# Tile h of one pair of chunks in the space of later sums, and a new order of the instructions from there on

## The chip, the cores and the metric

The kernel runs on one core of one Trainium2 chip. The metric is device time in microseconds. The engines are TensorE (PE, and PEld for its weight loads), VectorE (DVE), ScalarE (ACT), GpSimd (POOL) and SyncE (SP), which issues most transfers. All arithmetic of the products is in float32; the trace holds two records for most products.

## The reference

```python
def _attn_ref(q, k, v, a_re, a_im):            # 4 batches, 8 heads, 768 steps, 48 wide
    mag = np.sqrt(a_re * a_re + a_im * a_im)
    scale = np.minimum(mag, 0.999) / (mag + 1e-06)
    ...
    for t in range(S):
        new_re = ar * S_re - ai * S_im
        new_im = ar * S_im + ai * S_re
        S_re, S_im = new_re + k_t v_t^T, new_im
        y[:, :, t] = q_t @ S_re

def _moe_ref(x, U, V, w_ch1, w_ch2):           # x is y as (4, 768, 384); w_ch1 is 384 x 1536
    u = x + ((x^T @ U) @ V)^T                  # U is 768 x 32
    return u + np.maximum(u @ w_ch1, 0.0) @ w_ch2
```

A gated linear recurrence with complex gates is followed by a mixer over tokens of low rank and a mixer over channels.

## The kernel before, in words

The sequence of each of the four batches is cut into six chunks of 128 tokens. For every chunk the gates are turned into magnitudes and angles (`gates`), q and k are scaled and turned (`prep`, products `tr`), and the attention is computed in pieces (`chain`: products `inner`, `corners`, `dk`, `y`; states `G` and `GM`). Once a batch's six chunks are there, `mixer(m)` takes them as three pairs: m = 0, 1, 2 for the first batch, up to m = 11. A mixer multiplies by U (`rank`) and V (`mixed`), turns u (`uTp`, tile `uT`), forms the up products into tile `h` (1536 x 256 as 128 x 12 x 256), and the "down" products with w2.

There are three ways of doing the up products. For m = 0 they start before U's share is known, and six small products `fix` are then added to h by VectorE (`put_right`). For m = 1 and 2 they are plain (`up`, 36 products of 256 columns each). From m = 3 on they are done with fewer products (`up_fewer`, tile `few`) from sums of blocks of w1, which `combine` makes once, by thirteen VectorE additions of 128 x 512 (L1288): into seven slices of tile `sums` (`sums_w`, 128 x 3584 numbers) and one block of w1 itself. `down` serves m = 0 and `down_two`, with sums of halves of h in tiles `stage` and `more`, the others. Tile h is the single buffer `H_ALL` for all twelve pairs, as a ring of one: a pair's h may be written once the last one's is read for good.

Two steps stand around the place of the change. The weights come as raw words and are converted on the chip: for each of six pieces of w2 ScalarE makes two passes and VectorE three (L587, L400 on `w`, L589). Only then the "down" products of m = 0 that read that piece can run.

The order of all instructions is a table, `ORDER`: for each engine, kind of step and rank it gives the places in one common row of numbers. `plan.order()` sorts by it, and checks that nothing comes before what it needs and no buffer is taken early. A second table, `BANKS`, says which pair of PSUM banks each tile of sums uses. A third, `SPARE`, names places at which TensorE is given products of the identity with itself that nobody reads (L1528, in function `idle`), in units of 128 columns and at most three units to a product.

Of the kernel before, what the change touches and what calls it, by code (L numbers as in the profile page):

```python
# [30 lines left out]
    "TTTTTTTTTTTTTTTTTTAAAAYYYYTTAAAAYYYYTTAAAAYYYYTTAAAAYYYYTTTTTTTTTTAAAAYYYMTTAAAATYTYTTMMMMATAYTYATYMTYMMTYYTTATYTYMMYAYT"  # L31
    "YMTTYAMMMMTTATMTAAYTTATMAYTYAAYYMTTYTAYYTMTYTTAYMTATTYTAATYTMAAYTYAYTYTAYTYTYYYTAYMTTAMYYYAAMYYATTYYTTMTTAYYTMMYTTATYAMA"
    "AAMYTTMMTTTMMTAATAATMTAAYAYTAYAYTAYYTYAMTMYAYYMYAYTYAAMMAYTMYYYTMTYATMAMYATMYMTYTAYTAATAYAYYAAAATYTTAAYMYMYYMMTAAYMMAAYM"
    "TTMMMYYYMMYATYYAYTTYTYATAYTAATYYMTYMAAMTMTAMTATYMYTMAMTMMTYYTYAAYAYTATYTTYTTTYTATAYYTYYTAAMTYYYMMTAYTYTYAAAMTAYYMMTYYTT")
# [20 lines left out]
        ('ACT', 'gates'): {0: [1, 2, 4, 6, 7, 16, 17, 22, 23, 29, 28, 45, 70, 71], 1: [24, 27, 38, 39, 41, 42, 46, 47, 65, 64, 67, 68], 2: [129, 108,  # L55
# [10 lines left out]
        ('DVE', 'gates'): {0: [5, 8, 13, 18, 19, 54, 49], 1: [30, 21, 40, 43, 44, 51, 50], 2: [111, 143, 156, 185, 169], 4: [277, 322, 323, 372, 356],  # L66
# [10 lines left out]
        ('ACT', 'angles'): {0: [72, 86, 98, 100, 103], 1: [76, 106, 112, 114, 126], 2: [210, 231, 251, 240, 241, 242, 263, 269, 271], 4: [375, 395,  # L77
# [5 lines left out]
        ('DVE', 'angles'): {0: [81, 89], 1: [87, 107], 2: [211, 232, 252], 4: [376, 402, 425], 6: [581, 590, 591, 597, 617, 620, 660], 8: [695, 721,  # L83
# [167 lines left out]
def kernel(  # L251
# [812 lines left out]
    def mixer(m):  # L1064
# [120 lines left out]
        def c_of(n):  # L1185
            return "sums_w", n
# [411 lines left out]
```

## Time and profile before

| | |
|---|---|
| median of 3 runs | 617.83 us (615.37, 617.83, 617.84) |
| profiled execution | 616.25 us, span 614.5 us |
| TensorE busy | 597.1 us (97%) |
| VectorE busy | 531.4 us (86%) |
| ScalarE busy | 399.6 us (65%) |
| first `few` product of m = 3 | starts at 266.5 us |
| granted TensorE clock, mean | 0.999 |

A row of a timeline gives the start, the length of the merged records, the engine, the line, what is written from what, and how many records. A row of windows gives for each stretch its length, and for each engine the busy time and the number of its records, then the granted clock and the share and rate of the transfers. A row of waits gives who waited for whom, the total, how often, and the longest. TensorE's records overlap, so that the length of a merged row can be more than the distance to the next start.

### The profile page before, as it was taken

To read this page: it belongs to the slowest core of one execution; us is meant where nothing else is said; L and a number is where in the kernel's file an instruction comes from. 1 tells how busy PE (TensorE), PEld (TensorE's weight loads), DVE (VectorE), ACT (ScalarE), POOL (GpSimd) and SP (SyncE) were. 2 spreads that over 40 slices of the span, in tenths; PEclk is the share of its full clock that TensorE was granted. 3 is DMA by queue.
4 is the path that set the end of the run, shared out by engine and by line. 5 is a ranking of instruction groups with operands and counts; after the bars stand their busy time and mean duration, and the time that the engine had idled before them with its cause. 6 is when DMAs were issued, how large, how long until landed. Compare 5 with 4: busy or idle time off the path is not lost.

```text
span 614.5 us, 23950 instructions
## 1 busy us (share of the span) xinstructions
PE 597.1 (97%) x10572; PEld 526.5 (86%) x10572; DVE 531.4 (86%) x967; ACT 399.6 (65%) x789; POOL 36.9 (6%) x76
## 2 busy tenths in 40 slices
PE   6898989999999999999999999999999999999998
PEld 3566767666889889899999999899999998999997
DVE  6999999999999999999999999889699986464653
ACT  6999999888878898787686876574563532202020
POOL 4000000000000010010100000000100000000010
PEclk9999999999999999999999999999999999999999
DMA  9865556627233534441521522601122200000010
GB/s 212 196 149 119 135 119 153 161 61 151 62 60 69 105 67 75 78 98 27 112 53 22 106 50 45 125 11 29 36 59 47 56 11 19 14 8 7 7 39 26
DMA packets 173687, 45.77 MB, mean 74 GB/s; under 512 B 167632, under 2 KB 170384, under 8 KB 173584
## 3 DMA queue, kind: packets, MB, share of 16 engines
q1 hardware_dynamic: 171376, 39.90, 31.6%
q0 software_dynamic: 2208, 4.35, 2.1%
q8 instruction: 83, 1.36, 0.9%
q14 instruction: 20, 0.16, 0.1%
HBM read 33.59 MB, written 4.72 MB: 62 GB/s over the span
## 4 chain that ended last, share of the span: by engine, by line
PE 85%; ACT 7%; DVE 5%; DMA 1%; issue 1%; SPq 0%; DVEq 0%; ACTq 0%
PE down L1369 25%; PE few L1235 20%; PE up L1135 7%; PE dk L1009 4%; PE tr L873 4%; PE y L1048 4%; PE inner L923 3%; PE inner L920 2%; PE y L1040 2%; ACT gate L394 2%; PE tot L751 2%; PE mixed L1102 1%; PE up L1528 1%; PE uTp L1120 1%; PE corners L984 1%
## 5 line engine op out<-in xcount | busy, mean ns | idle before, releaser
L397 DVE TENSOR_TENSOR QK<-QK,T 96x512 f32<-96x512 f32 (+2 forms) x144 | 101.1, 723 | 4.8 <-ACT QK L884 2.3
L1369 PE MATMUL down<-w,h 128*128 128x192 f32 x396 | 72.1, 330 | 0.0
L1243 ACT COPY h<-few 128x512 f32<-128x512 f32 x54 | 31.1, 585 | 60.3 <-PE few L1235 60.2
L394 ACT ACTIVATE gate<-gate 128x768 f32<-128x768 f32 (+1 forms) x82 | 64.5, 796 | 4.9 <-DMA gate<-in_a_re_dram 1.8
L1369 PEld LDWEIGHTS down<-w,h 128*128 128x128 f32 x396 | 64.4, 190 | 1.3 <-issue 0.4
L884 ACT COPY QK<-tr 96x512 f32<-96x512 f32 x96 | 51.0, 586 | 14.2 <-PE tr L873 13.8
L400 DVE TENSOR_TENSOR xo<-down,xo 128x192 f32<-128x192 f32 (+1 forms) x79 | 29.8, 382 | 23.8 <-PE down L1369 23.5
L1135 PE MATMUL up<-uT,w 128*128 128x256 f32 x216 | 50.3, 385 | 0.0
L1235 PE MATMUL few<-stage,w 128*128 128x128 f32 x360 | 46.7, 277 | 0.0
L1135 PEld LDWEIGHTS up<-uT,w 128*128 128x128 f32 x216 | 40.0, 190 | 5.4
L1235 PEld LDWEIGHTS few<-stage,w 128*128 128x128 f32 x360 | 43.3, 192 | 0.3
L397 DVE TENSOR_TENSOR QKC<-qk,cs 128x768 f32<-128x768 f32 x44 | 41.6, 950 | 1.7 <-ACT cs L394 1.1
L1247 DVE CUSTOM_DVE_ANT_1 h<-few,h 128x512 f32<-128x512 f32 x54 | 35.8, 684 | 4.1 <-PE few L1235 3.1
L1235 PE MATMUL few<-stage,sums 128*128 128x128 f32 x288 | 37.4, 276 | 0.0
L400 DVE TENSOR_TENSOR h<-few,h 128x512 f32<-128x512 f32 x27 | 18.3, 685 | 21.7 <-PE few L1235 13.2
L1369 PE MATMUL down<-stage 128*128 128x192 f32 x198 | 36.8, 330 | 0.0
L1235 PEld LDWEIGHTS few<-stage,sums 128*128 128x128 f32 x288 | 35.2, 192 | 0.1
L989 ACT COPY AT<-corners 32x128 f32<-32x128 f32 x96 | 24.2, 255 | 14.9 <-PE corners L984 13.5
L788 POOL DMA_DIRECT2D gate<-F x15 | 12.1, 806 | 355.1 <-DVE F L817 203.1
L1369 PEld LDWEIGHTS down<-stage 128*128 128x128 f32 x198 | 32.3, 190 | 0.9 <-issue 0.6
L873 PEld LDWEIGHTS tr<-ident,QKC 64*96 64x96 f32 x768 | 24.0, 123 | 9.8 <-DVE QKC L397 3.3
L1311 POOL DMA_DIRECT2D out_dram<-xo x32 | 20.3, 677 | 190.3 <-DVE xo L400 112.4
(197 smaller groups left out, 1358.6 us busy)
## 6 DMA issues: line engine op xcount, KB each, us to landing
stage<-in_moe_w_ch_dram SPq DMA_DIRECT2D x12, 768.0 KB, 5.4
qk<-in_q_dram SPq DMA_DIRECT2D x24, 192.0 KB, 3.9
qk<-in_k_dram SPq DMA_DIRECT2D x24, 192.0 KB, 3.4
VP<-in_v_dram SPq DMA_DIRECT2D x24, 192.0 KB, 4.0
gate<-in_a_re_dram SPq DMA_DIRECT2D x22, 192.0 KB, 4.0
gate<-in_a_im_dram SPq DMA_DIRECT2D x22, 192.0 KB, 4.0
AT<-DG SPq DMA_DIRECT2D x96, 32.0 KB, 2.0
T<-E SPq DMA_DIRECT2D x48, 48.0 KB, 2.9
```

The source lines that it names most:

```text
L394: return nc.scalar.activation(out=o, in_=i, func=f, **kw)
L397: nc.vector.tensor_tensor(out=o, in0=a, in1=b, op=OP.mult)
L400: nc.vector.tensor_tensor(out=o, in0=a, in1=b, op=OP.add)
L873: nc.tensor.transpose(out=get(*ps[r])[0:DQ, h], in_=get(*qkc)[at, h * DQ:(h + 1) * DQ], identity=ident[at, at], tile_position=(r * HC, 0))
L884: nc.scalar.copy(out=to, in_=a)
L1009: nc.tensor.matmul(out=get(*dk[r])[x:x + w, h], lhsT=get(*ks)[at, h * DQ + x:h * DQ + x + w], rhs=get(*VPi)[at, h], start=True, stop=True, ...
L1048: nc.tensor.matmul(out=get(*y[u])[side(r, u), p], lhsT=k_of(h, r * HC, HC), rhs=get(*(mid_G if r else ("G", i - 1)))[:, h], start=False, s ...
L1135: nc.tensor.matmul(out=get(*ps)[:, e], lhsT=w1[:, f, (ff + e) * 128:(ff + e + 1) * 128], rhs=get(*uT)[:, f], start=(f == 0), stop=(f == KD ...
L1235: nc.tensor.matmul(out=get(*ps)[:, q], lhsT=w()[:, q * 128:(q + 1) * 128], rhs=v[0](), start=(n == 0 and q == 0), stop=True, skip_group_ch ...
L1243: ACT(c_act(n3 * CH) - 0.045, RU, lambda i=i, k=k: nc.scalar.copy(out=at(i, k), in_=get(*ps)), [ps], [o])
L1247: DVE(c_dve(n3 * CH), RU, lambda i=i, k=k: nc.vector._custom_dve(dve_ops.TENSOR_ADD_SAT, out=at(i, k), in0=get(*ps), in1=at(i, k), s0=math ...
L1369: nc.tensor.matmul(out=get(*to)[:, part], lhsT=x(j), rhs=y[:, j], start=(first and j == 0), stop=(j == KH - 1), skip_group_check=not first)
```

## The change

For m = 1 tile h becomes the first six of the seven slices of `sums` (3072 of 3584 numbers); all other pairs keep `H_ALL`. The sums of up weights can then be written only after h of m = 1 is no longer read, which the plan is told by a write of `("h", 1)` on three of the thirteen additions. And from the conversion of w2 on (place 505 of some 2770) the three tables are new: every engine's order, the banks and the spare products.

```diff
-        ring(h, "h", [H_ALL])
+        if m == 1:
+            ring(h, "h1", [sums_w.rearrange("p n m -> p (n m)")[:, 0:KF * N].rearrange("p (f t) -> p f t", t=N)])
+        else:
+            ring(h, "h", [H_ALL])
...
             def put(n, x, y, op, reads=()):
                 DVE(c_dve(n3), RC, lambda: nc.vector.tensor_tensor(out=c(n), in0=x(), in1=y(), op=op),
-                    [("w1", f) for f in range(KD)] + [c_of(k) for k in reads], [c_of(n)] + [("w1", 2, 0)] * (n == 7))
+                    [("w1", f) for f in range(KD)] + [c_of(k) for k in reads], [c_of(n)] + [("w1", 2, 0)] * (n == 7) + [("h", 1)] * (n in (0, 6) and not reads))
...
-        ('ACT', 'w2'): {0: [513, 507], 2: [575, 543], 4: [588, 602], 6: [630, 649], 8: [652, 655], 10: [707, 706]},
+        ('ACT', 'w2'): {0: [510, 517], 2: [546, 558], 4: [604, 600], 6: [650, 655], 8: [661, 659], 10: [698, 703]},
...
-         1, 352: 2, 436: 1, 592: 3, 604: 2, 614: 1, 627: 3, 640: 1, 643: 1, 647: 1, 662: 1, 685: 1, 712: 1, 719: 1, 724: 2}
+         1, 352: 2, 436: 1, 585: 3, 605: 2, 618: 3, 620: 1, 628: 1}
```

TensorE, from the spare product ahead of `fix` to the gate products that follow the first "down" products of m = 0 (`w_67` is w2, `ident` the identity of a spare product, GS the gates' logarithms in two parts). Before:

```order
L1528 MATMUL fix<-ident 128x128
L1174 MATMUL fix<-V,rw 128x256 x12
L1528 MATMUL down<-ident 128x384
L806 MATMUL ph<-GS_91,prefix_r 128x384
L806 MATMUL ph<-GS_92,prefix_r 128x384
L1326 MATMUL down<-w_67,h 128x384 x2
L1528 MATMUL ef ps<-ident 128x128
L1326 MATMUL down<-w_67,h 128x384 x6
L1528 MATMUL ef ps<-ident 128x128
L1326 MATMUL down<-w_67,h 128x384 x2
L1528 MATMUL ef ps<-ident 128x128
L1326 MATMUL down<-w_67,h 128x384 x2
```

And now:

```order
L1531 MATMUL ph<-ident 128x384
L806 MATMUL ph<-GS_91,prefix_r 128x384
L806 MATMUL ph<-GS_92,prefix_r 128x384
L1531 MATMUL fix<-ident 128x128
L1177 MATMUL fix<-V,rw 128x256 x12
L1531 MATMUL down<-ident 128x128
L1329 MATMUL down<-w_67,h 128x384 x10
```

The two `ph` products moved ahead of `fix`, ten "down" products stand in a row where twelve were broken up by four spare ones, and behind these rows the change has no spare product any more, where before there were four.

VectorE at the same place, from the first additions of `fix` to h on (`w_67` is w2 in conversion, `w_66` is w1, the rows on gate and GL belong to the next gates). Before:

```order
L1179 ISA h<-fix,h 128x512 x2
L654 ISA gate<-gate 128x768
L1179 ISA h<-fix,h 128x512
L587 TENSOR_SCALAR w_67<-w_67 128x768
L1288 TENSOR_TENSOR sums<-w_66 128x512
L1179 ISA h<-fix,h 128x512
L400 TENSOR_TENSOR gate<-gate 128x768
L1179 ISA h<-fix,h 128x512
L397 TENSOR_TENSOR qk<-qk,es 128x768
L673 SCALAR_TENSOR_TENSOR GL<-GL,gate 128x768
L400 ISA w_67<-w_67,stage 128x1536
L1288 TENSOR_TENSOR sums<-w_66 128x512
```

And now:

```order
L654 ISA gate<-gate 128x768
L1182 ISA h<-fix,h 128x512 x4
L400 TENSOR_TENSOR gate<-gate 128x768
L1182 ISA h<-fix,h 128x512
L687 TENSOR_SCALAR gate<-gate 128x768
L673 SCALAR_TENSOR_TENSOR GL<-GL,gate 128x768
L1182 ISA h<-fix,h 128x512
L587 TENSOR_SCALAR w_67<-w_67 128x768
L683 TENSOR_TENSOR GS_92<-GL,GS_91 128x768
```

The two sums of w1 are gone from here, and the additions to h stand closer together.

VectorE shortly before the first `few` product, the last additions of `combine` in the change (QKC are turned q and k, GM the middle state, `more` the halves of h for "down" of m = 2):

```order
L1291 TENSOR_TENSOR w_66<-w_66 128x512
L1291 TENSOR_TENSOR sums<-w_66,sums 128x512
L397 TENSOR_TENSOR QKC_95<-QKC_95,gate 128x768
L1364 TENSOR_TENSOR more<-h,more 128x384
L1291 TENSOR_TENSOR sums<-sums 128x512
L1291 TENSOR_TENSOR sums<-w_66 128x512
L817 SCALAR_TENSOR_TENSOR F<-F,ph 128x384
L397 TENSOR_TENSOR QKC_93<-qk,cs 128x768
```

Four of the thirteen stand in these rows; in the order before, the last one alone stood ahead of this row of `F`, the two before it some 10 and 20 rows further up.

More of the change, by code (lines that the diff above doesn't have):

```diff
@@ L95 @@
+        ('ACT', 'angles'): {0: [72, 86, 98, 100, 103], 1: [76, 106, 112, 114, 126], 2: [210, 231, 251, 240, 241, 242, 263, 269, 271], 4: [375, 395,
[5 rows of a table added]
+        ('DVE', 'angles'): {0: [81, 89], 1: [87, 107], 2: [211, 232, 252], 4: [376, 402, 425], 6: [582, 583, 584, 594, 614, 616, 658], 8: [694, 724,
[4 rows of a table added]
+        ('DVE', 'prep'): {0: [85, 104, 110], 1: [121, 128, 145], 2: [226, 250, 265], 3: [203, 304, 309], 4: [373, 424, 427], 5: [443, 470, 472], 6:
[6 rows of a table added]
         ('ACT', 'prep'): {0: [115, 117, 120, 122], 1: [158, 147, 154, 160], 2: [266, 270, 283, 281], 3: [319, 320, 327, 318], 4: [442, 439, 446, 445],
[4 rows of a table removed]
[4 rows of a table added]
@@ L100 @@
         ('DVE', 'rest'): {0: [118, 149, 155, 175, 159, 170, 194], 1: [174, 229, 234, 259, 209, 235, 248, 253], 2: [288, 315, 325, 366, 291, 314, 324,
[8 rows of a table removed]
-        ('DVE', 'levels'): {0: [123, 135, 148, 136, 137, 152], 1: [177, 192, 202, 195, 198, 225], 2: [292, 302, 308, 301, 303, 312], 3: [328, 371,
[9 rows of a table removed]
-        ('ACT', 'levels'): {0: [138], 1: [215], 2: [305], 3: [378], 4: [468], 5: [532], 6: [749], 7: [828], 8: [954], 9: [1035], 10: [1181], 11:
[2 rows of a table removed]
[8 rows of a table added]
+        ('DVE', 'levels'): {0: [123, 135, 148, 136, 137, 152], 1: [177, 192, 202, 195, 198, 225], 2: [292, 302, 308, 301, 303, 312], 3: [328, 371,
[9 rows of a table added]
@@ L122 @@
+        ('ACT', 'levels'): {0: [138], 1: [215], 2: [305], 3: [378], 4: [468], 5: [524], 6: [752], 7: [811], 8: [911], 9: [1033], 10: [1167], 11:
[2 rows of a table added]
         ('SP', 'place'): {0: [173, 199, 180, 181], 1: [249, 260, 244, 262], 2: [350, 349, 348, 347], 3: [415, 414, 418, 416], 4: [493, 500, 497, 499],
[4 rows of a table removed]
[4 rows of a table added]
         ('PE', 'rest'): {0: [157, 119, 127, 207, 208], 1: [254, 227, 230, 272, 274, 273], 2: [332, 294, 289, 358, 384, 380], 3: [428, 397, 400, 435,
[6 rows of a table removed]
-        ('ACT', 'rest'): {0: [191, 182, 200, 201, 219, 223, 222], 1: [255, 261, 256, 258, 280, 279, 278], 2: [342, 341, 336, 335, 385, 390, 391], 3:
[10 rows of a table removed]
@@ L145 @@
-        ('ACT', 'small'): {0: [600, 285, 307, 492, 396, 509, 601, 519, 610, 615], 1: [739, 799, 817, 811, 808, 864, 869], 2: [897, 910, 1046, 1061,
[4 rows of a table removed]
-        ('DVE', 'small'): {0: [246, 606, 623, 622, 633, 650, 678, 639, 692, 686, 787, 750], 1: [690, 703, 702, 877, 883, 896, 881, 917, 902, 944,
[29 rows of a table removed]
-        ('POOL', 'small'): {0: [859, 1056], 1: [1032, 1169, 1172], 2: [1314, 1403, 1460], 3: [1661, 1567, 1703], 4: [1952, 1876, 1885], 5: [2213,
-        2098, 2146], 6: [2207, 2214, 2266], 7: [2463, 2380, 2471], 8: [2549, 2509, 2728], 9: [2750, 2608, 2652], 10: [2713, 2694, 2703]},
@@ L182 @@
-        ('POOL', 'angles'): {6: [616], 8: [700, 756], 10: [874, 934], 12: [1072], 14: [1267, 1292], 16: [1495, 1547], 18: [1731], 20: [1913, 1977],
-        22: [2202, 2232]},
-        ('DVE', 'mixing'): {3: [637, 1027, 988, 1078, 1086, 659, 918, 754, 1098, 1103, 1221, 1247, 1288]},
[6 rows of a table added]
+        ('ACT', 'rest'): {0: [191, 182, 200, 201, 219, 223, 222], 1: [255, 261, 256, 258, 280, 279, 278], 2: [342, 341, 336, 335, 385, 390, 391], 3:
[10 rows of a table added]
+        ('ACT', 'small'): {0: [598, 285, 307, 492, 396, 509, 601, 525, 611, 621], 1: [710, 817, 806, 813, 802, 844, 854], 2: [912, 921, 1051, 1073,
[4 rows of a table added]
@@ new lines @@
+        ('DVE', 'small'): {0: [246, 608, 624, 625, 634, 648, 627, 641, 692, 691, 733, 744], 1: [690, 718, 688, 831, 884, 918, 869, 906, 907, 974, 995,
[29 rows of a table added]
+        ('POOL', 'small'): {0: [1025, 928], 1: [1150, 1090, 1212], 2: [1467, 1371, 1372], 3: [1631, 1672, 1690], 4: [1811, 1798, 1799], 5: [2030,
+        1963, 2214], 6: [2248, 2151, 2235], 7: [2403, 2329, 2469], 8: [2761, 2548, 2672], 9: [2705, 2605, 2699], 10: [2730, 2675, 2727]},
+        ('POOL', 'angles'): {6: [595], 8: [696, 763], 10: [852, 922], 12: [1087], 14: [1243, 1321], 16: [1444, 1543], 18: [1726], 20: [1958, 1997],
@@ L185 @@
+        22: [2169, 2273]},
+        ('DVE', 'mixing'): {3: [1011, 1045, 1020, 1063, 1068, 1069, 1125, 1208, 1245, 1271, 1281, 1285, 1288]},
 }
 SPARE = {20: 8, 32: 9, 62: 1, 66: 1, 73: 1, 82: 5, 91: 1, 113: 6, 116: 1, 119: 8, 140: 8, 153: 6, 157: 4, 167: 1, 168: 1, 207: 6, 216: 1, 217: 1, 282:
-         1, 352: 2, 436: 1, 592: 3, 604: 2, 614: 1, 627: 3, 640: 1, 643: 1, 647: 1, 662: 1, 685: 1, 712: 1, 719: 1, 724: 2}
+         1, 352: 2, 436: 1, 585: 3, 605: 2, 618: 3, 620: 1, 628: 1}
 class Plan:
```

9 lines of the change are left out of this document (4 added, 5 removed), and 240 rows, old and new, of the table ORDER.

## The prediction

> **What bounds the kernel now.** I read the page first: the span, the busy engines, and the chain of work that ended last.
>
> ```profile
> span 614.5 us, 23950 instructions
> PE 597.1 (97%) x10572; PEld 526.5 (86%) x10572; DVE 531.4 (86%) x967; ACT 399.6 (65%) x789; POOL 36.9 (6%) x76
> ```
>
> TensorE is busy for 597.1 of 614.5 us, so hardly a wait is left to take away. The question is where, after the point at which the order changes, TensorE does work that nobody needs or waits at all. The first moved row on TensorE is the row of `tot` products that the trace has at 104.2 us; the last of the first pair's "down" products ends at 154.6 us. I therefore cut the rest into stretches: to 154.6, to 182 (the second pair's up products), to 266 (up to the first `few` product), to the last product, and the tail.
>
> ```profile
> core 0: us, PE busy (x) PEld busy (x) DVE busy (x) ACT busy (x) POOL busy (x), PEclk, DMA share, GB/s
> 104.20:154.60 50.40, 49.71 (x655) 34.18 (x653) 47.82 (x74) 43.57 (x79) 2.47 (x3) 1.00 0.57 123
> 154.60:182.00 27.40, 26.92 (x507) 23.51 (x506) 26.39 (x40) 23.82 (x44) 1.39 (x2) 1.00 0.34 67
> 182.00:266.00 84.00, 83.96 (x1781) 75.02 (x1780) 82.21 (x145) 69.11 (x141) 6.88 (x10) 1.00 0.43 83
> 266.00:611.40 345.40, 344.99 (x5731) 329.05 (x5729) 278.20 (x545) 167.79 (x346) 19.42 (x32) 1.00 0.20 42
> 611.40:614.50 3.10, 0.05 (x1) 0.00 (x0) 0.36 (x1) 0.00 (x0) 0.00 (x0) 0.88 0.13 46
> ```
>
> The columns that matter are PE and DVE. From 266 us on TensorE is full (344.99 of 345.40) and VectorE has room (278.20): there the time is the sum of the products, which the change keeps. Up to 266 us both are nearly full: VectorE lacks 2.58, 1.01 and 1.79 us of the three stretches, 5.38 in all. So a saving on TensorE in the first stretch lasts to the end only if VectorE keeps up until 266 us.
>
> In the first stretch TensorE's 49.71 us hold the spare products of L1528, which fill places where it has nothing else to do:
>
> ```profile
> 104.20:154.60 50.40, 6.49 (x24) 4.00 (x24) 1.00 0.57 123
> L1528 PE MATMUL fix<-ident x4: 275/378/483, 118.9 to 123.7; 128*128 128x256 f32 x2, 128*128 128x128 f32 x2
> L1528 PE MATMUL tr<-ident x4: 273/275/356, 138.8 to 144.2; 128*128 128x128 f32 x4
> L1528 PE MATMUL inner<-ident x4: 276/378/382, 147.0 to 149.1; 128*128 128x128 f32 x2, 128*128 128x256 f32 x2
> ...
> 126.05 0.91 PE L1528 MATMUL down<-ident 128*128 128x384 f32 x2
> 126.65 0.67 PE L806 MATMUL ph<-GS,prefix_r 128*128 128x384 f32 x2
> ...
> 128.44 0.39 PE L1528 MATMUL ef ps<-ident 128*128 128x128 f32 x2
> 128.66 4.04 PE L1326 MATMUL down<-w,h 128*128 128x384 f32 x12
> ...
> 135.56 0.39 PE L1528 MATMUL ef ps<-ident 128*128 128x128 f32 x2
> 135.71 0.92 PE L699 MATMUL ef ps<-GS,fore 128*128 128x384 f32 x2
> ```
>
> The first row is that stretch with L1528 alone (PE, then PEld busy). There are 24 records, two to a product, so twelve products of 18 units of 128 columns. Durations overlap in the pipeline; what a spare product costs is the distance from its start to the next start: 0.22 us at 128.44, 0.15 at 135.56, 0.60 for the three units at 126.05.
>
> **The change, part by part.** *Spare products.* Up to the last "down" of the first pair, the two orders hold the same products on TensorE except for these: five are left, 3 + 2 + 3 + 1 + 1 = 10 units, so 8 units go. At 0.22 us each, the row at 128.44, that is **-1.8 us**; at the cheapest row (0.15) -1.2, and by the busy time (6.49 x 8/18) -2.9. I take 0.22 because most of those that vanish are of this one-unit kind. The gain is real only if the work that they waited for comes sooner by as much. That work is VectorE's: the conversion of w2 and the additions of `fix`. Two of the sums of up weights leave this stretch:
>
> ```profile
> 104.20:154.60 50.40, 1.38 (x2) 1.00 0.57 123
> 154.60:182.00 27.40, 0.68 (x1) 1.00 0.34 67
> 182.00:266.00 84.00, 6.79 (x10) 1.00 0.43 83
> ...
> 147.81 0.96 DVE L589 SCALAR_TENSOR_TENSOR w<-stage,w 128x768 uint32<-128x768 uint32 x1
> ...
> 151.83 2.85 PE L1326 MATMUL down<-w,h 128*128 128x384 f32 x8
> ```
>
> The first three rows are L1288 alone. With 1.38 us of sums gone, VectorE needs only 0.4 us of its 2.58 idle to be 1.8 earlier; and the last conversion ended at 148.77, 3 us ahead of the last four "down" products (151.83), so that part is covered.
>
> *The tile.* The second pair's h in `sums` costs no instruction; the same copies write it. It lets that pair's up products start before the first pair's "down" ends, and the third pair's start before the second's ends. In the new order the second pair's still come behind the first pair's last "down", and the third pair's come a few products sooner. TensorE is full there (83.96 of 84.00), so I price this at nothing: the cover is the products themselves, and with it gone it would be at most the 0.04 us of idle time.
>
> *The sums.* Three (1.38 + 0.68 = 2.06 us) leave the first two stretches, where h now lies, and come due before the first `few` at 266 us, behind the second pair's last use of h. VectorE's sum over the three stretches stays 156.42 us; the stretches shrink from 161.8 to 160.0, which leaves 3.6 us for its own waits:
>
> ```profile
> DVE h L1179 <- PE fix L1174: 0.9, 1, 0.9
> DVE gate L771 <- ACT gate L394: 0.4, 1, 0.4
> DVE w L400 <- ACT stage L394: 0.3, 1, 0.3
> DVE QK L397 <- PE inner L920: 0.2, 1, 0.2
> DVE rw L1151 <- PE rT L1149: 0.2, 1, 0.2
> ...
> DVE qk L397 <- DMA qk<-in_k_dram: 0.7, 1, 0.7
> DVE F L817 <- ACT F L394: 0.5, 1, 0.5
> DVE QK L397 <- ACT QK L884: 0.3, 1, 0.3
> DVE gate L654 <- ACT gate L394: 0.3, 1, 0.3
> ```
>
> These are VectorE's waits to 154.6 us and from there to 266 us: 3.8 us if all recur. It is 0.2 short, and I charge **+0.2**; the ends are 0 and all three sums on the path, +2.06. The sums themselves are not what `few` would wait for:
>
> ```profile
> 259.63 0.69 DVE L1288 TENSOR_TENSOR sums<-w 128x512 f32<-128x512 f32 x1
> ...
> 266.50 1.05 PE L1235 MATMUL few<-stage,sums 128*128 128x128 f32 x8
> ```
>
> The last sum was done 6.2 us ahead, three times what is added. What is queued behind the sums there, the turning of q and k and the copies of G, is what would be late next.
>
> *TensorE's waits.* The idle time is 0.69 + 0.48 us in the first two stretches, of which two waits are named:
>
> ```profile
> PE y L1048 <- DVE QK L397: 0.4, 1, 0.4
> PE rw ps L1158 <- DVE rw L1151: 0.4, 1, 0.4
> ```
>
> In the new order the `corners` products of the next chunk stand between `inside` and this `y`, so I take its wait off, **-0.3**. The other keeps a VectorE row of equal kind ahead of it and stays. The ends are -1.2 and 0. *Behind 266 us* the order is new but the products are the same: 0, with -0.4 (the idle 0.41) and +0.5 (an estimate: one more such wait) as ends. The tail of 3.1 us has the same last addition and the same transfers.
>
> The sum is -1.8 + 0.2 - 0.3 = -1.9, with ends at -4.5 and +1.4. Against the profiled execution's 616.25 us that is 614.3. The runs before stand at 615.37, 617.83 and 617.84, two levels with the profiled one between; a median of three may fall on either, so I add half of 617.83 - 616.25, 0.8: **615.1 us**.
>
> **The rivals.** *More comes back.* A busy TensorE may hide waits between records: PEld is busy for 34.18 of 50.40 us in the first stretch against 329.05 of 345.40 at the end. Then 2.9 for the spare products and 1.2 for all the idle time come back, -4.1: 612.2, or 612.9 with the half level. Against it: VectorE's 5.38 us of idle time caps it, and 3.8 of those are waits for others. [...]
>
> *Nothing comes back.* The spare products filled a wait for VectorE; without them TensorE waits as long. For it: in the first stretch VectorE is 47.82 of 50.40. Then only the 0.3 and the +0.2 are left: 616.2, or 617.0 on the same footing. Against it: the two sums that leave are VectorE's own time.
>
> *Slower: VectorE falls behind before 266 us.* The place is the third stretch, at whose end five of the thirteen sums now stand within 14 rows of VectorE's order, while TensorE has only the second and third parts of "down" to fill in. VectorE has 1.79 us free there and gets 2.06 of sums, and TensorE comes 1.8 sooner, so it is 2.1 late; and if each product `y` that needs G or its middle state waits 0.4, as the one above did (eleven of them in the six chunks, the first has no G), that adds 4.4. What they hold back, `rank`, `mixed` and `uTp`, opens the next up products, and no other work covers it. So 6.5 is lost against 2.1 gained: +4.4, 620.7, or 621.4. It decides once VectorE is later than the few us by which G was ahead of `y`. For it: VectorE's 82.21 of 84.00. Against it: it comes out of the first two stretches 2.06 us lighter.
>
> *The clock drops* where spare products are gone. For it speaks only what the same product took over the whole span, its slowest being the start:
>
> ```profile
> L1528 PE MATMUL tr<-ident x34: 272/484/1007, 1.4 to 144.2; 128*128 128x384 f32 x16, 128*128 128x128 f32 x14, 128*128 128x256 f32 x4
> ```
>
> The largest form took 1007 ns there; in the pair at 126.05 the two records together took 910. Twice the time on the 48 records of the first pair's "down" (0.32 us each, 4.04 us for 12 records above, less the overlap) is +15.4: 629.8, or 630.6. Against it: the granted clock is 1.00 in the first four stretches, and the place of the longest spare product quoted is 0.60 us wide. [...]
>
> **How the numbers follow.** The chances: forecast 0.53, more comes back 0.20, nothing 0.15, slower 0.10, the clock 0.02. A difference of 0.5%, 3.1 us of 617.83, is about what a measurement of this kernel can tell from no change, since its own runs differ by 2.5 us. Of the forecast's 0.53 I put 0.16 below 614.7 (the median falls on the lower level, 614.3 or under) and the rest within the bound. So faster is 0.16 + 0.20 = 0.36, the same 0.37 + 0.15 = 0.52, slower 0.12. The range, 612.2 to 618.3, goes from "more comes back" on the lower level to the end of the sum, 616.25 + 1.4 = 617.7, with most of the half level; about 0.08 lies below it and 0.12 above. The likeliest case alone spans 613.3 to 616.9: its sum with 1 us of play on the profiled level and on the median's.
>
> **What would show each step.** In the changed kernel's profile five spare products after 104 us, and the first pair's last "down" ending at 152.8 instead of 154.6, confirm the first term; an end at 154.6 with TensorE's waits on `fix` or w2 grown by as much is "nothing comes back". The first `few` product should start at 264.4 (266.5 less 2.1): earlier than 263 is "more", later than 266.5 is "slower", with waits of TensorE for QK, G or xo between 182 and 266. All thirteen sums should lie after the second pair's last product from `sums`, with VectorE over 98% busy in the third stretch. From the first `few` to the end it should still be 348.0 us (614.5 - 266.5); more than 1 us off makes the claim wrong that the rest only moves along. A clock under 1.00 between 104 and 182 us would show the last rival.

## The result and the profile after

| | kernel before | changed kernel |
|---|---|---|
| median | 617.84 us (615.37 to 618.9, 6 runs) | 613.45 us (611.94 to 614.29, 6 runs) |
| ratio | | 0.9934, 95% interval 0.9909 to 0.9958 |
| profiled execution | 616.25 us, span 614.5 us | 611.94 us, span 610.1 us |

Faster by 0.66%. The time lies inside the range that was forecast, but the gain is more than twice as large: 4.3 us between the profiled executions, against 1.9. Two repeats of the changed kernel's order, timed beside the kernel before, gave 0.9937 (0.9916 to 0.9958) and 0.9945 (0.9919 to 0.997).

The busy time on the changed kernel's page:

```profile
PE 594.4 (97%) x10558; PEld 525.9 (86%) x10558; DVE 530.8 (87%) x967; ACT 400.3 (66%) x789; POOL 36.6 (6%) x76
```

TensorE has 2.7 us less to do (594.4 against 597.1), VectorE 0.6. That alone isn't 4.3, so I cut the changed kernel's profile into stretches: from the first moved row on TensorE to the end of the first pair's last "down", from there to the first `few` product, and from there to the last product. The columns are those of the windows in the prediction.

```profile
102.79:150.50 47.71, 47.31 (x642) 32.81 (x640) 46.24 (x72) 44.20 (x79) 2.80 (x3) 1.00 0.58 130
150.50:261.56 111.06, 110.90 (x2288) 99.04 (x2288) 109.49 (x187) 94.08 (x187) 7.41 (x12) 1.00 0.40 78
261.56:607.10 345.54, 345.27 (x5730) 329.60 (x5726) 278.63 (x544) 167.02 (x344) 19.88 (x33) 1.00 0.20 42
```

The same three stretches of the kernel before, cut at the same rows:

```profile
104.18:154.61 50.43, 49.74 (x655) 34.21 (x654) 47.85 (x74) 43.59 (x79) 2.47 (x3) 1.00 0.57 123
154.61:266.50 111.89, 111.37 (x2289) 99.03 (x2289) 109.09 (x185) 93.42 (x186) 8.27 (x12) 1.00 0.41 80
266.50:611.45 344.95, 344.54 (x5728) 328.55 (x5726) 277.70 (x544) 167.29 (x345) 19.42 (x32) 1.00 0.20 42
```

From these rows the 4.3 us come apart: 104.18 - 102.79 = 1.39 are there before any moved row of TensorE runs, 2.72 come from the first stretch, 0.83 from the second, and the third gives 0.59 back. The third DVE column shows what happened in the first stretch. VectorE was busy for 47.85 us and idle for 2.58; now it is busy for 46.24 and idle for 1.47. Its work fell by 1.6 and its waits by 1.1, which is the whole 2.7. (The two parts of any engine add up to the stretch; TensorE's busy time fell by 2.43 and its idle time by 0.29. Which of the engines set the pace is not read from this row, but from the experiments.) VectorE's waits in the stretch are now these (before, they were the first five rows of waits in the prediction, the one for `fix` with 0.9 us at their head):

```profile
DVE F L817 <- ACT F L394: 0.8, 1, 0.8
DVE DG L935 <- PE inner L920: 0.2, 1, 0.2
```

### The profile page after: what moved, and what is told of

Same layout as the page of the kernel before. It is cut to its first block, busy times and chain, and to the rows that moved or that the text cites. A ratio compares the mean times of both kernels' runs of the same rounds, so it can differ in the third digit from the quotient of the medians.

```text
span 610.1 us, 23901 instructions
## 1 busy us (share of the span) xinstructions
PE 594.4 (97%) x10558; PEld 525.9 (86%) x10558; DVE 530.8 (87%) x967; ACT 400.3 (66%) x789; POOL 36.6 (6%) x76
## 3 DMA queue, kind: packets, MB, share of 16 engines
q8 instruction: 83, 1.36, 1.0%
## 4 chain that ended last, share of the span: by engine, by line
PE 74%; DVE 12%; ACT 8%; issue 2%; DMA 2%; SPq 1%; DVEq 0%; ACTq 0%
PE down L1372 21%; PE few L1238 20%; PE up L1138 6%; PE tr L873 3%; PE y L1048 3%; PE dk L1009 3%; PE inner L923 2%; ACT gate L394 2%; DVE QK L397 2%; DVE QKC L397 2%; PE inner L920 2%; PE y L1040 2%; PE rank L1083 1%; PE tot L751 1%; DMA gate<-in_a_im_dram 1%
## 5 line engine op out<-in xcount | busy, mean ns | idle before, releaser
L1372 PE MATMUL down<-w,h 128*128 128x192 f32 x360 | 64.9, 329 | 0.0
L1372 PEld LDWEIGHTS down<-w,h 128*128 128x128 f32 x360 | 58.5, 190 | 1.2 <-DVE h L1250 0.4
```

Of the source, the lines that this page charges most:

```text
L1372: nc.tensor.matmul(out=get(*to)[:, part], lhsT=x(j), rhs=y[:, j], start=(first and j == 0), stop=(j == KH - 1), skip_group_check=not first)
```

## The experiments

Each row of this table is read from the profile of one: the start of the first row after the unmoved part, the length of the first stretch, of the second, and from the first `few` product to the start of the last TensorE row.

| kernel | time against before | first row | first stretch | second | third |
|---|---|---|---|---|---|
| before (first profile) | | 104.18 | 50.43 | 111.89 | 343.81 |
| before, again | 1.0001 (0.9979 to 1.0022) | 104.61 | 50.45 | 111.76 | 343.84 |
| before without spare products | 1.0048 (1.0025 to 1.0071) | 105.12 | 50.71 | 112.34 | 346.87 |
| the same, twelve products more at the start | 1.0019 (0.9997 to 1.0041) | 103.62 | 51.34 | 111.90 | 343.63 |
| before, sums late | 1.0012 (0.999 to 1.0034) | 104.44 | 50.03 | 112.55 | 344.75 |
| before, sums late, no spare products | 1.0051 (1.003 to 1.0073) | 104.84 | 49.68 | 112.69 | 348.55 |
| before, one gate row first | 1.0006 (0.9988 to 1.0024) | 104.25 | 51.41 | 111.90 | 343.98 |
| before, gate row first, sums late | 1.0016 (0.9999 to 1.0033) | 104.05 | 50.85 | 112.89 | 343.61 |
| changed (first profile) | 0.9934 (0.9909 to 0.9958) | 102.79 | 47.71 | 111.06 | 344.41 |
| changed, again | 0.9937 (0.9916 to 0.9958) | 102.75 | 47.74 | 111.10 | 344.17 |
| changed, eight slices | 0.9945 (0.9919 to 0.997) | 103.28 | 47.72 | 110.95 | 344.30 |
| changed without spare products | 0.9942 (0.992 to 0.9965) | 103.80 | 47.26 | 110.99 | 344.30 |
| the same, five products more at the start | 0.994 (0.9914 to 0.9965) | 103.96 | 48.96 | 110.95 | 344.26 |
| changed, two sums early | 0.9989 (0.9969 to 1.0009) | 106.89 | 48.77 | 110.94 | 344.55 |

### Both kernels once more

The kernel before, unchanged:

> The kernel before, unchanged, as a second witness. Theory A (the 1.4 us by which the changed kernel was ahead at its first moved row on TensorE is chance of a run): this profile's row of tot products, at 104.18 us in the first profile, lies somewhere between 102.5 and 105, and the span moves by the same amount. Theory B (it belongs to the changed code): 104.2 within 0.2 us. Both: ratio 1.000 within 0.003.

And the changed kernel:

> The changed kernel once more. If the 1.4 us that it was ahead already at its first moved row (102.8 us against 104.2) are the level of one run, that row may start anywhere from 102.8 to 105; if they belong to this kernel, it starts at 102.8 again, within 0.3 us, and the TensorE wait on no other instruction in the `inner` products near 95 us is again 0.7 us where the kernel before had 1.0 to 1.6. Either way the stretch from that row to the end of the first pair's last down products is 47.7 us and the stretch from the first few product to the end 348.5 us, each within 0.3; the time is 613.5 us, ratio 0.993 to 0.995.

The three stretches repeat within 0.3 us (rows 1, 2, 9, 10 and 11 of the table), so they belong to the kernels: the change is worth -2.7, -0.8 and +0.5, together 3.0 us. The first 104 us don't repeat so well over all the profiles: 102.75 to 106.89. Of the runs whose mean granted clock was 0.999 or more, 36 of the kernel before took 616.14 us on average and 11 of the changed order 613.19: again 3.0. The medians of all runs, 98 and 21, are 616.6 and 613.0 us, 3.6 apart. The further 1.4 us of the profiles lie where no row of TensorE moved. A wait for nothing that the profile shows is 0.63 us of it, in all four profiles of the two kernels after the same record of the `inner` products. TensorE's timeline there, the kernel before:

```profile
94.35 0.61 PE L920 MATMUL inner<-QK 96*16 96x16 f32 x55
96.29 0.24 PE L920 MATMUL inner<-QK 96*16 96x16 f32 x9 [1.33 <-issue]
```

The changed kernel in its first profile:

```profile
95.13 0.24 PE L920 MATMUL inner<-QK 96*16 96x16 f32 x9 [0.70 <-issue]
```

And in its second:

```profile
95.09 0.24 PE L920 MATMUL inner<-QK 96*16 96x16 f32 x9 [0.20 <-issue]
```

The kernel before had 1.04 us there in its second profile, and the changed one without spare products 1.79. Another 0.46 us are there at 13 us already, behind a row of spare products at the start that both kernels have, here in the first profiles, before and changed:

```profile
10.42 3.40 PE L1528 MATMUL tr<-ident 128*128 128x384 f32 x6
10.36 3.00 PE L1531 MATMUL tr<-ident 128*128 128x384 f32 x6
```

In the second profiles this row took 3.94 and 3.59 us. So both pieces differ from run to run at least as much as between the kernels, and the 1.4 us are not shown to be the change's.

### The spare products taken out of the kernel before

```diff
-         1, 352: 2, 436: 1, 592: 3, 604: 2, 614: 1, 627: 3, 640: 1, 643: 1, 647: 1, 662: 1, 685: 1, 712: 1, 719: 1, 724: 2}
+         1, 352: 2, 436: 1}
```

> The kernel before without its twelve spare products behind 104 us (18 units of 128 columns, 4.3 us from start to next start), nothing else. Theory 'they are in the way': TensorE goes on at once and the first pair's down ends about 4 us sooner, ratio 0.993. Theory 'they only fill': TensorE waits in their places for VectorE's additions of fix and conversions of w2, the last down product still starts at 151.8 counted from the tot row at 104.2, ratio 1.000. I expect between them, -1 to -2 us, ratio 0.997 to 0.998, since the price in the sum (-1.8 for 8 units) supposed that VectorE can follow.

All twelve are gone, 18 units, which at the prediction's 0.22 us would be 4 us. The first stretch became 0.26 us longer than in the second profile of the kernel before. Where TensorE had been busy with them it now waits; the stretch:

```profile
105.12:155.83 50.71, 46.07 (x632) 30.83 (x630) 47.61 (x75) 43.54 (x79) 2.48 (x3) 1.00 0.56 122
```

And the first five of TensorE's waits in it:

```profile
PE ph L806 <- DVE h L1179: 1.2, 1, 1.2
PE ef ps L699 <- DVE GS L683: 0.8, 1, 0.8
PE rT L1149 <- ACT r L1089: 0.6, 1, 0.6
PE rw ps L1158 <- DVE rw L1151: 0.6, 1, 0.6
PE fix L1174 <- ACT rw L1163: 0.5, 1, 0.5
```

PE is busy 3.67 us less, and not one microsecond of it comes back. A few tenths are hidden by a late transfer in this run, which heads VectorE's waits in the stretch:

```profile
DVE GS L799 <- DMA gate<-F: 1.7, 1, 1.7
```

That transfer took 4.7 us from its issue (3.6 in the kernel before), and the first addition to h began 1.84 us after the first `fix` product, where it begins 1.21 us after it in the kernel before. An estimate from these rows: without the 0.6 us the stretch would be 50.1, 0.3 less than with the spare products. The next kernel, which lacks them too and has no such wait, confirms it: 51.34 less a wait of 1.31 us of another kind is 50.0. So the spare products were cover for waits on VectorE and ScalarE, and cost 0.3 to 0.4 us in place of 4. Why the whole kernel is 0.5% slower shows mainly in the third stretch, 3 us longer with the same products in the same order. TensorE's waits from 260 us on, in the same kernel, name two for nothing shown that the kernel before does not have:

```profile
PE inner L923 <- issue: 1.7, 1, 1.7
PE mixed L1102 <- issue: 0.7, 1, 0.7
```

### The same number of products, elsewhere

If these waits depend on how many TensorE instructions stand ahead, twelve products more at the start must move them back. Two spare places in the first microseconds were cut into one-unit products and a third one finer (the columns stay the same, twelve products more):

```diff
-            out += [-1] * SPARE.get(at[n], 0) + [n]
+            out += [{20: -2, 32: -2, 82: -3}.get(at[n], -1)] * SPARE.get(at[n], 0) + [n]
...
+            step = {-2: 1, -3: 2}.get(n, AHEAD)
...
-            idle(min(run, AHEAD))
-            run -= min(run, AHEAD)
+            idle(min(run, step))
+            run -= min(run, step)
```

> The kernel before without its twelve spare products behind place 436, as in the run that took 619.7 us, but with the same columns of spare products in the first 40 us cut into twelve more products, so that everything behind the first pair's down products has as many TensorE instructions ahead of it as in the kernel before. Theory 'instruction supply by position': the waits on no other instruction of 0.5 to 1.7 us at 194, 422 and 469 us vanish, the stretch from the first few product to the end is 348.0 us again (351.0 without them), and the time is 617.3 us. Theory 'the spare products keep something up that lasts' (clock, or a lead over VectorE): the stretch stays at 351 us and the time at 619.7 us.

The two waits vanished, and the third stretch is 343.63 us again. The time is 618.05 us, 0.2% from the kernel before instead of 0.5%: the theory of position holds for the 3 us. The first stretch is longer than without the move (51.34); a wait of this kind, 1.31 us, turned up in front of `dk` at 111 us, and more than explains it.

### The sums late, in the order before

```diff
-        ('DVE', 'mixing'): {3: [637, 1027, 988, 1078, 1086, 659, 918, 754, 1098, 1103, 1221, 1247, 1288]},
+        ('DVE', 'mixing'): {3: [987.3, 1027, 988, 1078, 1086, 917.3, 918, 1087.5, 1098, 1103, 1221, 1247, 1288]},
```

> The kernel before with the three early sums of up weights (VectorE, 2.06 us) moved behind, to between the second and third pair's work, all other rows in their old order and all spare products kept. Theory 'VectorE sets the pace up to 154 us': the first stretch gets shorter by up to 1.2 us (two sums at 0.6 us from start to next start) although TensorE's rows are the old ones, and what comes back is partly paid again before 266 us; ratio 0.998 to 1.000. Theory 'the spare products set it': nothing, ratio 1.000, since they stand in TensorE's row whether it waits or not.

The first stretch shrank by 0.42 us, and the second grew by 0.8: VectorE has two rows of sums more there (the third sum moved within it), and they delay what stands behind them. The third was 0.9 us longer in this profile; 0.46 of it is a wait for nothing shown, the rest was not followed up. In the old order moving the sums gains nothing. The same without spare products:

> Both at once: the three sums late and the twelve spare products gone, the rest in the old order. Theory 'VectorE sets the pace': more than the sum of the two single edits, up to -4 us, ratio 0.9935, as the place of the spare products is only free once VectorE is earlier. Theory 'they are in the way': the same as without spare products alone.

Here the first stretch is 49.68 us. Against the 50.71 with the sums early and no spare products either that is 1.0 less, but 0.6 of it is the late transfer of that run; here the same wait for `gate<-F` is 0.3 us. Against the 50.0 or 50.1 without it, moving the sums is worth about 0.4, as with the spare products, so the two edits together give no more than the sum of the two. The second stretch takes it back (112.69), and the third has the 1.7 us of waits in front of `inner` again. Behind that wait the granted clock fell to a half, and TensorE's busy time in the third stretch is 1.75 us longer than without spare products alone (345.68 against 343.93):

```profile
468.60:472.00 3.40, 3.40 (x12) 3.40 (x12) 3.40 (x8) 1.75 (x4) 0.00 (x0) 0.50 0.02 5
```

### Two sums early, in the changed order

The tile of sums gets an eighth slice, so that these two sums stay clear of the second pair's h:

```diff
-    sums_w = singles.tile([128, 7, KF // 3 * 128], FP, name="sums")
+    sums_w = singles.tile([128, 8, KF // 3 * 128], FP, name="sums")
...
-            return sums_w[:, n] if n < 7 else w1[:, 2, 0:KF // 3 * 128]
+            return sums_w[:, (6, 0, 1, 2, 3, 4, 7)[n]] if n < 7 else w1[:, 2, 0:KF // 3 * 128]
...
-        ('DVE', 'mixing'): {3: [1011, 1045, 1020, 1063, 1068, 1069, 1125, 1208, 1245, 1271, 1281, 1285, 1288]},
+        ('DVE', 'mixing'): {3: [637.5, 1045, 1020, 1063, 1068, 659.5, 1125, 1208, 1245, 1271, 1281, 1285, 1288]},
```

> The changed kernel with two of the thirteen sums of up weights back on VectorE among the additions of fix, where the kernel before had them (h of the second pair then lies in six slices of an eight-slice tile that these two sums do not touch; TensorE's order and its spare products are those of the change). Theory 'VectorE sets the pace up to the last down products': that stretch grows by 0.7 to 1.4 us, from 47.7 to 48.4-49.1, since two sums are 1.38 us of VectorE; if the lighter work before 266 us gives that back, the time is 613.5, if not 614.5. Theory 'VectorE has room there' (the prediction: 2.58 us idle): the stretch stays 47.7 within 0.3 and the time 613.5 us.

And the control, with the eight slices and the sums where the change has them:

> The changed kernel with the eight-slice tile of the run with two early sums, and all thirteen sums where the change has them: the control for that run (every engine's order is that of the change). Theory 'VectorE sets the pace up to the last down products': that stretch is 47.7 us again, within 0.3, where two sums put back made it 48.8. If the layout of the tile were what counted, it would be 48.8 here too. The run with the early sums also stood 3.4 us above the changed kernel in its median, of which its stretch explains 1.1: if the rest comes from the layout, this one stands at 614.5; if it is the level of the first 104 us, which no part of the change touches, at 612.1 to 613.5.

The first stretch with the sums early:

```profile
106.89:155.66 48.77, 48.06 (x643) 32.73 (x641) 47.36 (x74) 44.69 (x79) 2.81 (x3) 1.00 0.56 126
```

And the control's:

```profile
103.28:151.00 47.72, 47.31 (x642) 32.79 (x641) 46.21 (x71) 44.17 (x79) 2.80 (x3) 1.00 0.57 129
```

VectorE has 1.15 us more to do and the stretch is 1.05 longer; the idle time of VectorE (1.41 against 1.51) hardly moved. The slices themselves do nothing. And the second stretch has the same length with eleven sums to do as with thirteen: in the new order the late sums really are free there. This is the clearest piece of the gain: 1.05 us, about a third of the 3.0. The early-sums kernel is slower by more than that in its median; its profile lost some 4 us already before the first moved row. A wait of 1.26 us for `xo` and a lower clock behind it, 1.4 us (in the section on the hardware), are parts of that; the rest is not explained, nor whether the early sums have to do with it.

### One row of VectorE moved in the order before

The order before makes VectorE wait 0.9 us for `fix`; the change puts the gates' pass of L654 in front of the additions to h, and the wait is gone. That one row alone:

```diff
-        6: [456, 480, 485, 501, 510, 568, 502], 8: [629, 645, 653, 661, 680, 663], 10: [770, 788, 793, 802, 832, 861], 12: [949, 967, 984, 991, 1024,
+        6: [456, 480, 485, 501, 510, 568, 502], 8: [621.5, 645, 653, 661, 680, 663], 10: [770, 788, 793, 802, 832, 861], 12: [949, 967, 984, 991, 1024,
```

> The kernel before with one row of VectorE moved: the gates' pass of L654 ahead of the first addition of fix to h, as the change has it; TensorE's order is untouched. Theory 'VectorE's work and its waits set the pace up to the last down products': the wait of 0.9 us for fix is filled, the stretch goes from 50.4 to 49.5-49.9 us, and the first few product starts 0.5 to 0.9 us sooner; time 616.0 us. Theory 'TensorE sets it there' (the prediction's first term): the additions to h come up to 0.95 us later, the down products wait for them or the spare products no longer cover it, and the stretch stays at 50.4 or grows to 51; time 616.5 to 617.5 us.

With the sums late as well:

> As the run before this, and the three early sums moved late too (TensorE's order untouched, spare products kept). Theory 'VectorE sets the pace': less work (1.38 us) and less waiting (0.9 us) add up, and the stretch is 48.2 to 49 us where the change has 47.7; with the sums late alone it was 50.0. Whether it lasts to the first few product depends on VectorE's waits between 155 and 266 us, where the late sums alone gave their 0.4 us back: time 615.5 us if it lasts, 616.5 if not. Theory 'TensorE sets it': 50.0 us as with the late sums alone.

Both expectations of "VectorE sets the pace" missed: the first stretch grew, to 51.41 and 50.85 us (0.96 and 0.82 more than without the row moved). The timeline around the row in the first of these kernels, ScalarE and VectorE:

```profile
123.66 0.63 ACT L1163 COPY rw<-rw ps 128x256 f32<-128x256 f32 x2 [0.66 <-PE rw ps L1158]
124.19 0.84 ACT L394 ACTIVATE gate<-gate 128x768 f32<-128x768 f32 x1
125.49 0.84 ACT L394 ACTIVATE gate<-gate 128x768 f32<-128x768 f32 x1 [0.45 <-DVE GS L801]
126.36 0.96 DVE L654 CUSTOM_DVE_ANT_0 gate<-gate 128x768 f32<-128x768 f32 x1 [0.91 <-ACT gate L394]
127.24 1.88 DVE L1179 CUSTOM_DVE_ANT_0 h<-fix,h 128x512 f32<-128x512 f32 x3
```

The longest of TensorE's waits in that stretch:

```profile
PE ph L806 <- DVE h L1179: 1.6, 1, 1.6
```

The row had nothing to read yet. ScalarE makes its input after the copies of `rw`, so VectorE waits for the gate instead of for `fix`, h comes later, and TensorE's `ph` products wait 1.6 us for h. (In the first of the two kernels VectorE waited 1.2 us for a transfer for `GS` too; the second had no such wait.) In the changed kernel ScalarE's order moved as well; the same place in its timeline:

```profile
122.43 0.35 ACT L1166 COPY rw<-rw ps 128x256 f32<-128x256 f32 x1
122.85 0.84 ACT L394 ACTIVATE gate<-gate 128x768 f32<-128x768 f32 x1
123.60 0.35 ACT L1166 COPY rw<-rw ps 64x256 f32<-64x256 f32 x1
123.72 0.96 DVE L654 CUSTOM_DVE_ANT_0 gate<-gate 128x768 f32<-128x768 f32 x1
124.77 2.48 DVE L1182 CUSTOM_DVE_ANT_0 h<-fix,h 128x512 f32<-128x512 f32 x4
```

The gate's pass stands between the two copies of `rw`; it is done when VectorE wants it, VectorE fills the time in which `fix` is made, and then adds four times without a stop. So VectorE's idle time is no reserve of its own: it is the seam between three engines. That it closed because rows of ScalarE, VectorE and TensorE moved together is read from these rows; no run here moves two of the three alone, so the share of each is not shown.

### The spare products taken out of the change

```diff
-         1, 352: 2, 436: 1, 585: 3, 605: 2, 618: 3, 620: 1, 628: 1}
+         1, 352: 2, 436: 1}
```

> The changed kernel without its five spare products (10 units of 128 columns) behind place 436; what they compute is read by nobody. Theory 'products cost TensorE time' (the first term of the prediction): the stretch up to the last down products is 2.2 us shorter (the distance from start to next start of the five) and the time 611.3 us. Theory 'they only fill': that stretch stays at 47.7 within 0.4 us, with TensorE's named waits (for fix, w2, GS) longer by about 2 us in all; the time is 613.5 us. Theory 'instruction supply': as 'they only fill', but five products fewer stand ahead of everything that follows, so waits on no other instruction appear at other places behind 266 us, and the stretch from the first few product to the end grows from 348.5 to as much as 351.5: up to 616.5 us.

The first stretch is 0.48 us shorter (47.26) where the start distances of the five sum to 2.2. The time is 0.9942, no different from the change's own. Here five products fewer ahead of the third stretch didn't lengthen it. With five products more at the start, by cutting the first spare place into single units:

```diff
-            out += [-1] * SPARE.get(at[n], 0) + [n]
+            out += [-2 if at[n] == 20 else -1] * SPARE.get(at[n], 0) + [n]
...
+            step = 1 if n == -2 else AHEAD
...
```

> The changed kernel without its five spare products, with five more products at the start (the columns of the first spare place cut finer), so that everything behind the down products has as many TensorE instructions ahead of it as in the change. Theory 'they only fill': the stretch up to the last down products is 47.3 us, as it was without them (47.7 with them). Theory 'instruction supply by position': ten records more stand ahead of the `inner` products near 95 us, so the wait on no other instruction that the changed kernel has there (0.2 to 1.8 us in three profiles) moves ten records forward or vanishes; if it vanishes, the time is 611 us, else 612 us. If position does not matter, the wait stays in front of the same record.

The wait near 95 us did not vanish, but it moved as the theory of position has it. Five products are ten records, and it now stands ten records earlier among the 64: after 45, with 19 to come, where the changed kernel has it after 55 with 9 to come.

```profile
94.94 0.53 PE L920 MATMUL inner<-QK 96*16 96x16 f32 x45
96.22 0.32 PE L920 MATMUL inner<-QK 96*16 96x16 f32 x19 [0.75 <-issue]
```

The first stretch missed its expectation, 48.96 us instead of 47.3; the reason is the clock, below. The median (0.994) is that of the change. None of these kernels is faster than the change.

## Why the prediction was right, and where it was not

**What bounds the kernel.** Right in its first half: the third stretch is TensorE's (345.27 of 345.54 us busy), the same products in another order, and it stayed within the 1 us that was allowed it (344.95 to 345.54; the 0.6 us more, 0.5 over all profiles, were not followed up). And the cap "only if VectorE keeps up until 266 us" was the right place to look.

**The step that failed** is the first term, "8 units go. At 0.22 us each ... that is -1.8 us". It took TensorE's spare time for a price. Taking twelve out of the old order gave back 0.3 to 0.4 us in place of 4, taking five out of the new one 0.5 in place of 2.2. Units do not carry the term; what goes with the 2.7 us of the first stretch is VectorE's column, work 1.6 and waits 1.1 less. The prediction had these rows, 47.82 of 50.40, and used them only as a condition ("VectorE needs only 0.4 us of its 2.58 idle to be 1.8 earlier"), not as the sum. That column alone would have given 2.3 of the 2.7 without any spare product: two sums leave (1.38 by its rows), and the wait of 0.9 for `fix` closes. Of these the experiments show the sums, 1.05 us; that the closed wait is most of the rest is read from the rows.

**The sums.** Forecast +0.2, with 0 to +2.06 as ends, for their arrival ahead of the first `few`. In the old order the ends were right: the second stretch grew by 0.8 when they came. In the new one it shrank by 0.8, and two sums more or less made no difference to it. What keeps it open lies in the new order around them, which was not taken apart. All thirteen run from 202.4 to 255.0 us, behind the second pair's last product from `sums` (197.65), and VectorE is busy for 109.49 of 111.06 us, 98.6%, over what were the prediction's second and third stretch: these two marks were as foretold.

**TensorE's waits.** Forecast -0.3 for the wait of `y` on QK; it is gone, and TensorE's idle time in the second stretch fell from 0.52 to 0.16 us (111.89 - 111.37 and 111.06 - 110.90). Right, and small; the other 0.5 of the 0.8 us by which that stretch shrank is busy time of TensorE and was not followed up.

**The tile** was priced at nothing by itself; it was not tried alone, since without the new order nothing uses it.

**The rivals.** The first `few` product starts at 261.56 us, "earlier than 263", which was the mark of "more comes back", and its 612.2 to 612.9 us is nearer to 613.45 than the forecast. Its reason was another: it gave the time to the spare products' 2.9 us and to waits hidden inside a busy TensorE, and the runs show neither. "Nothing comes back" had the cause right, the spare products filled waits for VectorE, and the conclusion wrong, since the change shortened the waits themselves. "Slower" showed its mechanism in small, 0.8 us of the second stretch, where the sums were moved in the old order. "The clock drops" did not happen where the changed kernel's rows moved (1.00 in all three stretches); it was seen in three other profiles, once with the five spare products gone from their places, once with them still there.

**The range** held, and that was partly luck. The first term had the wrong cause; that another, VectorE's lighter work and shorter waits, gave 2.7 us in the place of its 1.8 was not foreseen. The 1.4 us by which the profiles differ ahead of everything that moved on TensorE were in no term either; without them the time would be some 614.9 us, inside the range and nearer to 615.1. A slip without weight: the mark of 264.4 us for the first `few` product takes off 2.1 and leaves out the +0.2 of the sum.

## What to carry to other kernels

Price a change from the column of the engine that the stretch waits for, its work and its idle time, and not from filler on the engine that looks busiest: filler that covered waits gave back 0.3 to 0.4 us in place of 4 when it went, and here the wait did not close when one row was moved alone. Moving work to a later stretch pays when that stretch's order leaves room for it; three sums moved late were worth nothing in the old order, and two of them 1 us in the new. Before an experiment is read, look for what happened in that run alone: one late transfer of 0.6 us made a gain of 0.4 look like 1.0. And when runs of kernels differ by a few microseconds, cut the profile at common rows and look first at the part that nothing touched.

## What the runs showed of the hardware

**TensorE's waits for nothing shown go by position.** Mostly in groups of very short products (55 records in the 0.61 us of the row near 95 us) TensorE waited 0.2 to 1.8 us for nothing that the profile shows: after the same record in the kernels with as many products ahead, ten records earlier with ten more ahead, and in other groups (1.66 us near 469 us) with 24 fewer. Two kernels had no such wait near 95 us: the one with two sums early, which had waited 1.26 us for `xo` just before, and the kernel before with twelve products more at the start, where a position 24 records earlier would still lie in the group. The page of the changed kernel counts the transfers that carry instructions:

```profile
q8 instruction: 83, 1.36, 1.0%
```

That is 1.36 MB in 83 packets, some 16 KB each. The times of these packets in the traces go with the waits: in the kernel before one landed at 95.04 us and TensorE went on at 96.29; in the changed kernel's first profile at 93.75 and 95.13, in its second at 93.80 and 95.09. The waits were 1.33, 0.70 and 0.20 us, but from the landing to the next record it was 1.25, 1.38 and 1.29. Of the 28 waits for "issue" in TensorE's timelines of the fourteen profiles, 26 end 1.25 to 1.54 us after a packet has landed; the two others are of 0.16 and 0.20 us. In the kernel before with twelve products more at the start the packet had landed at 93.45 us, 1.6 us ahead of the group near 95. That TensorE waited for its instructions, as long as the packet came late, is read from these distances and from the runs in which the waits moved with the number of products ahead; no view here names the engine that a packet is for, and what made it late was not looked into.

**The clock dropped after short waits.** In the changed kernel with its five spare products moved to the start, the granted clock fell to 0.52 for some 3 us (columns as above):

```profile
118.00:121.00 3.00, 1.76 (x20) 1.03 (x16) 3.00 (x5) 2.56 (x4) 0.96 (x1) 0.91 0.48 88
121.00:124.00 3.00, 3.00 (x22) 0.79 (x16) 2.93 (x6) 2.14 (x3) 0.00 (x0) 0.52 0.50 155
```

The same time in the kernel with the five just removed:

```profile
118.00:121.00 3.00, 1.82 (x22) 1.15 (x20) 3.00 (x6) 2.72 (x5) 0.96 (x1) 1.00 0.43 80
```

The 24 records of `rw ps` took 4.45 us in the former and 2.77 in every other profile, which is the 1.7 us by which that first stretch missed; its row of the timeline:

```profile
120.47 4.45 PE L1161 MATMUL rw ps<-w,rw 128*32 128x512 f32 x24 [0.64 <-DVE rw L1154]
```

The named waits ahead of it were 0.60 and 0.64 us, and with nearly the same 3 us ahead of it the other profile kept 1.00. The kernel with two sums early shows the same between 94 and 97 us (0.57), after 3 us in which TensorE was busy for 1.40 and the clock was already 0.87, and the kernel before with sums late and no spare products behind the wait of 1.66 us near 468 us (the same wait with the sums early left the clock at 1.00). An estimate from these windows, with the clock at a half as long as it is down: (0.09 + 0.48) x 3 / 0.5 = 3.4 us in the first kernel, (0.13 + 0.43) x 3 / 0.5 = 3.4 in the second, and in the third the 3.40 us of its row at 0.50. So the clock fell behind waits of 0.60 and 0.64 us close together, of 1.26 and 0.35, or a single one of 1.66, in some runs and not in others, for 1.7 us here and 1.4 there (12 records of `up` in 4.26 us instead of 2.86). The length of a wait alone doesn't tell it either: in the first profile of the changed kernel the clock was 0.50 from 8.76 to 12.17 us, where TensorE had been idle for 3.75 us until 8.95; in that of the kernel before it was 1.00 there, with 3.82 us idle until 9.02. What decides it is not shown, nor whether the spare products are of use against it: the medians with and without them (0.9942 and 0.994 against 0.9937) don't tell.
